# Loading the last w2 row in two partition ranges, without an early write of the output: a decode layer on one Trainium2 core

## The chip, the cores and the metric

The kernel runs on one core of a Trainium2 chip. The metric is the device time of one execution in microseconds, the median of several runs. Beside it there is one profiled execution, from which all durations and positions below are taken.

## The reference

One token each for two batch rows (B = 2, D = 576). The row is normalised, an attention over the last 2048 positions of a cache and a squared-ReLU MLP work on the same normalised row, and both results are added to the input. All tensors are bf16.

```python
xn = layernorm(A_x)                                    # [2, 1, 576]
q  = xn @ wq                                           # 32 heads of 128
p  = softmax(q . k_cache[:, :, -2048:] * 128 ** -0.5)  # 16 kv heads, 2 query heads each
a  = (p . v_cache[:, :, -2048:]) @ wo                  # [4096 x 576]
h  = relu(xn @ w1 + b1) ** 2                           # 4608 wide
m  = h @ w2 + b2                                       # w2: [4608 x 576]
out = A_x + a + m                                      # [2, 1, 576]
```

With two rows there is next to no reuse of weights or cache: 53.6 MB go from HBM to SBUF once, and 2.3 KB come back.

## The kernel before

All large loads are issued by SP, in one order written out by hand: wq, then the k and v tiles of eight units of work (four kv heads of one batch row each, 2 MB a tile), w1 among them, then wo and w2. A load is [128 partitions x n], and each partition's n elements are contiguous in HBM. For each unit the kernel transposes k on TensorE, computes scores, a softmax, and the product with v; the MLP's first half runs when w1 is there (`mlp_h`), and leaves its result transposed in `hT_sb`.

w2 has 4608 rows. They are split into two halves (x = 0, 1) of 128 x 18: partition p holds 18 consecutive rows (FR = 18) of each half, one row being 576 elements or 1152 bytes. The first half is loaded whole into `w2a_sb` (L440), of the second half rows 0 to 8 into `w2b_sb` (L441) and rows 9 to 17 into `w2c_sb` in three pieces given by `W2P`: rows 9 to 14, rows 15 and 16, and row 17 (L442 and L443). All of these are issued by SP between 96 and 101 us. Ahead of them on the queue are the last v tiles and wo, and behind them on SP is only half of the output. A transfer may have to wait before its issue until the one that used its semaphore before has landed.

The end of the kernel is the sum for the output. TensorE accumulates it in `out_ps` (rows 0 and 1: columns 0 to 287; rows 32 and 33: columns 288 to 575): the products with wo, with w2a, then with w2b (18 matmuls), three matmuls into `spin_ps` whose result is not used, and 18 matmuls with w2c. Two matmuls belong to each row of the 18. The first matmul on each piece of w2c waits for that piece.

ScalarE then casts `out_ps` to bf16 (`fin_sb`, L478), and two transfers of [2 x 288] write it out: columns 0 to 287 from ScalarE's queue (L479), columns 288 to 575 from SP's (L480). Ahead of the cast ScalarE issues one more transfer (L477): it writes two partitions of `w2b_sb` to the columns 0 to 287 of the output, as soon as w2b has landed. The real write of L479 goes to the same place and waits until the early one has landed.

Of the kernel before, what the change touches and what calls it, by code (L numbers as in the profile page):

```python
# [16 lines left out]
def kernel(  # L17
# [14 lines left out]
    nc = tc.nc  # L32
    P = 128
    B, Sq, D = A_x.shape
# [39 lines left out]
    FR = L1 // P  # L74
    assert HW == 32 * FR and QH * 2 == NC and NC * WC == 32
    W2P = [(9, 15), (15, 17), (17, 18)]
    R9 = 9
    HD = D // 2
    RO = 32 + B
    RP = 96 + B  # L80
# [11 lines left out]
    def matmul(*a, **k):  # L92
        tc.keep_in_program_order(nc.tensor.matmul(*a, **k))  # L93
# [5 lines left out]
    out2d = out.rearrange("b s d -> (b s) d")  # L99
# [80 lines left out]
    for t0, half, k0, n, pc in ((0, 0, 0, NK, 0), (0, 1, 0, NK, 1), (1, 0, 1, NK - 1, 1), (1, 1, 0, NK - 1, 0)):  # L180
# [11 lines left out]
                          in_=own[:].unsqueeze(2).to_broadcast([P, NC, WC]))  # L192
# [11 lines left out]
                          in_=ident[0:2 * NG4, 0:2 * NG4].rearrange("p (x g) -> p x g", g=NG4).unsqueeze(3)  # L204
# [3 lines left out]
    w2_rows = B_w2.rearrange("(x p r) n -> x p (r n)", x=2, r=FR)  # L208


    w2c_sb = w2pool.tile([P, (FR - R9) * D], BF16, name="w2c")

    out_ps = psum.tile([RO, HD], F32, tag="out", name="out_ps")
    nc.vector.memset(out_ps[:], 0.0)

    def out_acc(lhsT, rhs, o, start=False, stop=False, acc=out_ps, base=0):
        for i in range(2):
            p = base + 32 * i
            matmul(acc[p:p + B, :], lhsT=lhsT, rhs=rhs[:, o * D + i * HD:o * D + (i + 1) * HD], start=start,
                   stop=stop, skip_group_check=True, tile_position=(0, p))  # L220
# [167 lines left out]
    def step(u):  # L388
        fin = None
        w = u - 2  # L390
        with_pv = w >= 0
        for g in range(NG):
            transposes(u, g)
            if with_pv and g == 1:
                pv(w, 0, 2)
            if with_pv and g == 2:
                pv(w, 1, 2)
                fin = pv_end(w)
            if g == TG + 1:
                scores(u, 0)  # L400
            if g == TG + 2 and fin:
                fin()
        scores(u, 1)
        softmax(u)

    def pv_all(u):
        pv(u, 0, 1)
        pv_end(u)()
# [29 lines left out]
    w2a_sb = w2pool.tile([P, FR * D], BF16, name="w2a")  # L438
    w2b_sb = kvpool.tile([P, R9 * D], BF16, tag="kv", name="w2b")
    nc.sync.dma_start(out=w2a_sb[:], in_=w2_rows[0])  # L440
    nc.sync.dma_start(out=w2b_sb[:], in_=w2_rows[1, :, 0:R9 * D])  # L441
    for r0, r1 in W2P:  # L442
        nc.sync.dma_start(out=w2c_sb[:, (r0 - R9) * D:(r1 - R9) * D], in_=w2_rows[1, :, r0 * D:r1 * D])  # L443
    step(NU - 1)
    pv_all(NU - 2)
    pv_all(NU - 1)
    pre_ps = psum.tile([RP, HD], F32, tag="sc", bufs=2, name="pre_ps")
    nc.vector.memset(pre_ps[:], 0.0)
    pre_sb = work.tile([P, HD], F32, tag="t1", name="pre_sb")
    nc.gpsimd.memset(pre_sb[:], 0.0)  # L450
# [17 lines left out]
    for r in range(FR):  # L468
        w, o = (w2b_sb, r) if r < R9 else (w2c_sb, r - R9)
        out_acc(hT_sb[:, 1, r, :], w, o, stop=(r == FR - 1))  # L470
        if r == R9 - 1:
            for _ in range(3):
                matmul(spin_ps[0:B, :], lhsT=ws[:, 0, :], rhs=wo_sb[:, 0:512], start=True, stop=True,
                       skip_group_check=True)

    fin_sb = work.tile([RO, HD], BF16, tag="fin", name="fin_sb")
    nc.scalar.dma_start(out=out2d[:, 0:HD], in_=w2b_sb[0:B, 0:HD])  # L477
    nc.scalar.copy(out=fin_sb[:], in_=out_ps[:])  # L478
    nc.scalar.dma_start(out=out2d[:, 0:HD], in_=fin_sb[0:B, :])  # L479
    nc.sync.dma_start(out=out2d[:, HD:D], in_=fin_sb[32:RO, :])  # L480
# [30 lines left out]
```

## Time and profile before

| What | Value |
|---|---|
| Time, median of 3 runs | 133.66 us (133.63 to 133.71) |
| Profiled execution | 133.6 us, span 131.7 us |
| TensorE busy | 84.6 us (64% of the span) |
| VectorE busy | 63.1 us (48%) |
| ScalarE busy | 46.6 us (35%) |
| Read from HBM | 53.62 MB, 407 GB/s over the span |
| SP's queue (q1) | 95.6% of the 16 DMA engines' time |
| Mean granted TensorE clock | 0.883 |

The span runs from the first to the last instruction of the core. The DMA lines count what the core's 16 DMA engines did; q1 is SP's queue, q10 ScalarE's, and q8 and q14 bring instructions. "Landing" is the update of a transfer's semaphore, which each engine that took part in the transfer makes once. In the lists, "PE" is TensorE, "PEld" its weight loads, "ACTq" and "SPq" the issuing sides of ScalarE and SP.

### The profile page before, as it was taken

The numbers are of one execution on the slowest core, as the hardware profiler recorded it, in microseconds if no ns is written. First come the engines' busy times: TensorE is split into PE (matmuls) and PEld (weight loads), VectorE is DVE, ScalarE is ACT, GpSimd is POOL, SyncE is SP. The second block draws the span as 40 slices with busy tenths as digits, with TensorE's granted clock in tenths as the row PEclk, the third lists the DMA queues.
The fourth block names the chain that finished last, engine by engine and source line by source line (L and its number), as shares of the span: only waits on it lengthen the run. The fifth ranks groups of instructions, "written<-read, shape, count | busy, mean of one in ns | idle before, by whom it ended". The sixth has DMA issues, their size and how long they took to land.

```text
span 131.7 us, 2025 instructions
## 1 busy us (share of the span) xinstructions
PE 84.6 (64%) x818; PEld 46.3 (35%) x818; DVE 63.1 (48%) x176; ACT 46.6 (35%) x68; POOL 4.2 (3%) x14
## 2 busy tenths in 40 slices
PE   0040767985599687699687797003919974629782
PEld 0010236553346353345353353002507631205341
DVE  6760034555447677457677496400073487560000
ACT  6700019497255185265085283200015452000101
POOL 2000000010100100100100100100010001000000
PEclk9999999999779999859999999955586899655799
DMA  4999999999999999999999999999999989899970
GB/s 118 480 419 420 418 443 418 448 418 423 445 413 438 423 443 428 413 458 413 443 423 411 458 490 403 408 431 428 413 443 418 504 381 504 382 416 403 400 286 1
DMA packets 3643, 53.74 MB, mean 408 GB/s; under 512 B 418, under 2 KB 563, under 8 KB 819
## 3 DMA queue, kind: packets, MB, share of 16 engines
q1 hardware_dynamic: 3604, 53.61, 95.6%
q8 instruction: 6, 0.10, 0.3%
q10 hardware_dynamic: 30, 0.02, 0.0%
q14 instruction: 3, 0.02, 0.0%
HBM read 53.62 MB, written 0.00 MB: 407 GB/s over the span
## 4 chain that ended last, share of the span: by engine, by line
DMA 74%; PE 15%; ACT 5%; issue 1%; SPq 1%; DVE 1%; ACTq 0%; DVEq 0%
DMA w<-in_B_w_dram 24%; DMA w2c<-in_B_w_dram 23%; DMA k<-in_A_k_cache_dram 17%; DMA wq<-in_A_wq_dram 10%; PE kT_ps L96 5%; PE h_ps L93 3%; ACT kT L273 3%; PE q_ps L93 2%; PE sc_ps L93 2%; PE o_ps L93 1%; PE out_ps L93 1%; ACT L305 1%; SPq L120 1%; DVE qrow L241 1%; ACT qrow L241 0%
## 5 line engine op out<-in xcount | busy, mean ns | idle before, releaser
L96 PE MATMUL kT_ps<-ident_f,k 128*128 128x128 f32 x256 | 39.0, 295 | 6.7 <-DMA k<-in_A_k_cache_dram 4.2
L273 ACT COPY kT<-kT_ps 128x1024 bf16<-128x1024 bf16 x32 | 31.8, 1012 | 15.3 <-PE kT_ps L96 15.3
L96 PEld LDWEIGHTS kT_ps<-ident_f,k 128*128 128x128 f32 x256 | 29.3, 149 | 21.8 <-issue 7.4
L275 DVE COPY kT<-kT_ps 128x1024 bf16<-128x1024 bf16 x32 | 21.8, 682 | 6.4 <-PE kT_ps L96 5.9
L93 PE MATMUL sc_ps<-kT,qz 128*32 128x512 bf16 x128 | 9.8, 384 | 6.1 <-DVE kT L275 5.5
L305 ACT ACTIVATE p<-sc_ps,bias 128x512 bf16<-128x512 f32 x8 | 5.5, 687 | 21.5 <-DVE gown L301 21.4
L93 PE MATMUL o_ps<-v,pT 128*32 128x512 bf16 x128 | 12.2, 466 | 0.0
L93 PE MATMUL h_ps<-w,xnT 128*4 128x288 bf16 x72 | 4.5, 442 | 8.8 <-DMA w<-in_B_w_dram 8.8
L93 PEld LDWEIGHTS <-xnT 128*4 128x4 bf16 x108 | 3.5, 117 | 18.3 <-issue 15.3
L336 DVE SCALAR_TENSOR_TENSOR o<-o_ps,in_s,o 128x128 f32<-128x128 f32 x24 | 8.2, 344 | 0.4
L308 DVE STREAM_TRANSPOSE pT<-p 128x512 bf16<-128x512 bf16 x8 | 5.7, 709 | 5.6 <-ACT p L305 5.6
L376 DVE TENSOR_TENSOR hrow<-t 100x1152 bf16<-100x1152 f32 x2 | 2.6, 1354 | 10.5 <-ACT t L374 10.5
L93 PE MATMUL q_ps<-wq,xnT 128*4 128x512 bf16 x36 | 4.2, 622 | 5.4 <-DMA wq<-in_A_wq_dram 4.0
L294 DVE TENSOR_REDUCE m<-sc_ps 128x1 f32<-128x512 f32 x8 | 5.5, 691 | 3.4 <-PE sc_ps L93 3.4
L93 PE MATMUL op_ps<-o,of_h 128*32 128x129 f32 x16 | 3.4, 299 | 4.6 <-DVE o L336 4.6
L298 POOL PARTITION_ALL_REDUCE gmax<-m x8 | 2.9, 365 | 92.2 <-DVE m L296 92.2
L93 PEld LDWEIGHTS <-qz 128*32 128x32 bf16 x128 | 2.0, 94 | 9.9 <-DVE kT L275 7.6
L334 DVE TENSOR_SCALAR o<-o_ps,in_s 128x128 f32<-128x128 f32 x8 | 2.7, 343 | 5.3 <-PE o_ps L93 5.3
L96 PE MATMUL pro_ps<-ident,xn_sb 2*128 2x2 bf16 x5 | 0.9, 181 | 6.8 <-DVE xn_sb L171 6.5
L241 ACT CAST qrow<-q_ps 100x512 bf16<-100x512 f32 x1 | 0.6, 585 | 12.1 <-DVE qrow L241 12.1
L463 ACT COPY pre_sb<-pre_ps 34x288 f32<-34x288 f32 x1 | 0.4, 393 | 12.6 <-PE pre_ps L93 12.6
L93 PE MATMUL out_ps<-wo,ws 128*2 128x288 bf16 x32 | 4.0, 441 | 1.1 <-DVE ws L352 1.1
(76 smaller groups left out, 61.4 us busy)
## 6 DMA issues: line engine op xcount, KB each, us to landing
k<-in_A_k_cache_dram SPq DMA_DIRECT2D x8, 2048.0 KB, 25.6
v<-in_A_v_cache_dram SPq DMA_DIRECT2D x8, 2048.0 KB, 22.8
w<-in_B_w_dram SPq DMA_DIRECT2D x1, 5184.0 KB
wo<-in_A_wo_dram SPq DMA_DIRECT2D x1, 4608.0 KB
wq<-in_A_wq_dram SPq DMA_DIRECT2D x1, 3584.0 KB, 12.9
w2a<-in_B_w_dram SPq DMA_DIRECT2D x1, 2592.0 KB
w2b<-in_B_w_dram SPq DMA_DIRECT2D x1, 1296.0 KB, 29.2
wq<-in_A_wq_dram SPq DMA_DIRECT2D x1, 1024.0 KB, 4.8
```

The source lines that it names most:

```text
L93: tc.keep_in_program_order(nc.tensor.matmul(*a, **k))
L96: tc.keep_in_program_order(nc.tensor.transpose(*a, **k))
L241: cp(out=qrow[:, k * QW:(k + 1) * QW].rearrange("p (i a d) -> p i a d", a=2, d=Dh), in_=q_ps[0:RB, k * QW // 2:(k + 1) * QW // 2].rearrang ...
L273: nc.scalar.copy(out=kT, in_=kT_ps[:])
L275: nc.vector.tensor_copy(out=kT, in_=kT_ps[:])
L294: nc.vector.tensor_reduce(out=m1[:], in_=sc_ps[:], axis=AX.X, op=ALU.max)
L298: nc.gpsimd.partition_all_reduce(gmax[:], m2[:], channels=P, reduce_op=ReduceOp.max)
L305: nc.scalar.activation(out=p_sb[:], in_=sc_ps[:], func=ACT.Exp, bias=bias[:, 0:1], scale=scale, accum_out=o1[:, Dh:Dh + 1])
L308: nc.vector.transpose(out=pT[:].rearrange("p j r -> p (j r)"), in_=p_sb[:])
L334: nc.vector.tensor_scalar(scalar1=in_s[:, 0:1], scalar2=None, op0=ALU.mult, **kw)
L336: nc.vector.scalar_tensor_tensor(scalar=in_s[:, k:k + 1], in1=o1[:, 0:Dh], op0=ALU.mult, op1=ALU.add, **kw)
L376: nc.vector.tensor_tensor(out=h4[:, :, k * HB:(k + 1) * HB], in0=t4, in1=t4, op=ALU.mult)
```

## The change

Row 17 of w2c, the last piece, is loaded by two transfers: partitions 0 to 57 and partitions 58 to 127. The other pieces stay as they are. The early write of the output (L477) is left out, so ScalarE issues one transfer less and its write of the output waits for the cast alone.

```diff
     W2P = [(9, 15), (15, 17), (17, 18)]
     R9 = 9
+    PE2 = 58
...
     for r0, r1 in W2P:
-        nc.sync.dma_start(out=w2c_sb[:, (r0 - R9) * D:(r1 - R9) * D], in_=w2_rows[1, :, r0 * D:r1 * D])
+        cols = slice((r0 - R9) * D, (r1 - R9) * D)
+        for p0, p1 in ((0, PE2), (PE2, P)) if r1 == FR else ((0, P),):
+            nc.sync.dma_start(out=w2c_sb[p0:p1, cols], in_=w2_rows[1, p0:p1, r0 * D:r1 * D])
...
     fin_sb = work.tile([RO, HD], BF16, tag="fin", name="fin_sb")
-    nc.scalar.dma_start(out=out2d[:, 0:HD], in_=w2b_sb[0:B, 0:HD])
     nc.scalar.copy(out=fin_sb[:], in_=out_ps[:])
```

In the order of the built program the lists of VectorE and GpSimd are the same as before. SP has one more transfer (58 x 576 and 70 x 576 in place of 128 x 576), and ScalarE one less. On TensorE the order is the same; the first matmul on row 17 waits for the 58 partitions, and the weight load ahead of it for the 70.

## The prediction

> **What bounds the kernel now.** I read the chain that ended last first. Its last pieces, from 95 us on, end in the transfers of w2c:
>
> ```profile
> 96.95 30.81 DMA w2c<-in_B_w_dram
> 127.75 0.04 issue
> 127.80 1.36 PE out_ps L93 x18
> 129.16 0.02 issue
> 129.18 0.39 ACT fin_sb L478
> ```
>
> The reader should see that nothing but weights holds the end: transfers, 18 matmuls on w2c, one ScalarE copy, output. The chain hides one thing: the 18 matmuls have three waits, one for each piece of w2c. In the trace the last two start at 128.85, right behind the last landing of the last piece (128.81), and everything after that is fixed: the copy at 129.18, the two output transfers at 129.60.
>
> ```profile
> 125.71 0.25 ACTq L477 DMA_DIRECT2D out_dram<-w2b  x1
> 129.18 0.39 ACT L478 CAST fin_sb<-out_ps 34x288 bf16<-34x288 f32 x1 [4.37 <-PE out_ps L93]
> 129.60 0.32 SPq L480 DMA_DIRECT2D out_dram<-fin_sb  x1
> 129.60 0.25 ACTq L479 DMA_DIRECT2D out_dram<-fin_sb  x1
> ```
>
> ScalarE's output transfer lands at 130.71, SP's at 130.89, and the span ends at 131.7 behind SP's. So a delay of the last landing of w2c moves the end one for one. Next I asked how full the transfer engines are while that last piece comes in:
>
> ```profile
> core 0: us, PE busy (x) PEld busy (x) DVE busy (x) ACT busy (x) POOL busy (x), PEclk, DMA share, GB/s
> 126.00:126.60 0.60, 0.60 (x16) 0.43 (x12) 0.00 (x0) 0.00 (x0) 0.00 (x0) 1.00 1.02 409
> 126.60:127.10 0.50, 0.50 (x10) 0.29 (x5) 0.00 (x0) 0.00 (x0) 0.00 (x0) 1.00 0.70 275
> 127.10:127.60 0.50, 0.50 (x3) 0.12 (x2) 0.00 (x0) 0.00 (x0) 0.00 (x0) 1.00 0.46 176
> 127.60:128.10 0.50, 0.34 (x7) 0.23 (x7) 0.00 (x0) 0.00 (x0) 0.00 (x0) 1.00 0.37 141
> 128.10:128.50 0.40, 0.40 (x10) 0.29 (x7) 0.00 (x0) 0.00 (x0) 0.00 (x0) 1.00 0.22 78
> ```
>
> The last two columns are the point: the share of the 16 DMA engines falls from all of them to about half at 127.1 and a fifth at 128.3. The engines do not finish together. The trace records every DMA packet, and packets follow each other on an engine without a gap, so the end can be laid out in 16 rows. Each engine moves 8 rows of the last piece, 1152 bytes each, one every 47.0 ns. Eight engines end them between 126.65 and 127.04 us. The other eight end at 127.53, 127.59, 128.09, 128.24, 128.31, 128.42, 128.44 and 128.48. The lag comes from instruction blocks:
>
> ```profile
> q8 instruction: 6, 0.10, 0.3%
> q14 instruction: 3, 0.02, 0.0%
> ```
>
> Six blocks of 16 KB and two of 8 KB (the third record of q14 is a small one) are fetched between 28.9 and 123.3 us. Before the first, 16 landings of one transfer lie within 0.4 us (28.22 to 28.64). After it one of 16 is 1.5 us behind (35.00 against at most 33.49), and each further block makes one more engine late: by about 0.75 us for 8 KB, 1.25 to 1.7 for 16 KB.
>
> **Part 1, the last row in two transfers.** How many engines does a transfer use? Every transfer lands once for each engine: 128 rows give 16 landings, the 4-row loads of b1 give 4, the 2-row transfers 2, the 1-row load of b2 1. In all of them each engine has the same number of rows. I take equal shares as the rule for the new ones. 58 is 2 x 29, so 58 rows in equal shares fit on 2 engines at most (of 16); 70 is 14 x 5, so 70 rows go on 14. The trace names no engines, and I assume that transfers on two engines always have the same two, which the 14 include.
>
> The Trainium skill says the same in "DMA: Bandwidth & Descriptors", section "Why a DMA increments its semaphore by 16 and not by 1": the engine count is the largest number up to 16 that divides the slowest dimension, and on this path the lowest-numbered engines are taken. By it 58 goes on engines 0 and 1, and 70 on 0 to 13; no transfer of 58 or 70 rows is in the trace to agree or not.
>
> So two engines have 29 + 5 = 34 rows of the last piece instead of 8, twelve have 5, two have none. Which two get 34? The early write of the output is a 2-row transfer, and its packets show them. One is at 126.764 us, directly behind the packet that ends the last piece on an engine that is on time (126.76); the other is at 127.534, directly behind the end at 127.53 us. So one of the two is on time, and the other is the least late of the eight.
>
> - The late one of the two: 26 rows more x 0.047 = 1.22 us, and one more semaphore write, 0.006 us. 127.53 + 1.23 = 128.76 us. From the last byte to the landing the trace has 0.28 to 0.38 us, 0.30 on this engine. Landing at 129.06 (129.04 to 129.14).
> - The on-time one: 126.76 + 1.23 = 127.99 us, covered.
> - The other late ones: 3 rows less x 0.047 = 0.14 us. 128.48 - 0.14 = 128.34 us, landing at 128.67. No longer last.
>
> The last landing goes from 128.81 to 129.06: **+0.25 us** (0.23 to 0.33). The gain of 0.14 us on the twelve is paid for and lost, because the two that take over the work have only one free member.
>
> The additional transfer costs SP one more issue, 0.33 to 0.43 us by the row of line 443, at about 97 us; nothing is queued behind it on SP but the final output at 129.60, and the queue then holds 25 us of work. Cost nothing. On TensorE the last row now has two waits, one on a weight load (70 rows, landing 128.67) and one on the matmul behind it (58 rows). Nothing else is queued there, and the weight load is under the longer wait. Rows 15 and 16 keep their landing, 128.46, and their four matmuls end before 129.
>
> **Part 2, no early write.** It is issued in 4.4 us of ScalarE idleness (the bracket in the second fence), and its packets (29 + 9 ns) come after the last piece on both engines. Removing it frees nothing on the path. The final write of ScalarE also no longer waits for its landing at 128.00; that wait was over before 129.60. Gain: none.
>
> What may be lost is a warmed path. ScalarE's final write goes from packet to landing in 0.36 us; the early pair took 0.47, and SP's final one 0.49. If ScalarE's becomes like these, it lands 0.12 later, at 130.83, still ahead of SP's 130.89: nothing. The far bound is the first transfer that queue makes, the load of x: 1.49 us from issue to landing, against 1.11 for the final write. That is 0.38, less 0.18 of cover by SP: 0.20 us. I take 0.03, near the first, since the early write's issue (0.25 us) was no longer than the final one's.
>
> **Sum.** +0.25 + 0.03 = +0.28 us. The profiled execution took 133.6 us, 0.06 below the median of the runs, 133.66; the sum gives 133.88 for it and 133.94 for the median. That is 0.21%, just about the 0.2% (0.27 us) that a measurement of this kernel can tell from no change.
>
> **Rivals.**
> 1. *Blocks fall on other engines, and the two are on time.* That each block is tied to a fixed engine is not shown; the trace is one execution. If both of the two end their 8 rows before 128.34 - 1.23 = 127.11 us, the split does only good: every late engine has 3 rows less, the last landing is 0.14 earlier, 133.52 us. For it: 8 of 16 engines are on time. Against: the TensorE and VectorE programs, which need most blocks, keep their length (1217 rows and 152), and the runs of before lie within 0.08 us.
> 2. *Blocks of 16 KB fall on one of the two.* Then 34 rows begin on an engine that ends at 128.09 to 128.48: 129.32 to 129.71, +0.8 to +1.2 us, 134.5 to 134.9. The same against it.
> 3. *The halves are spread over all engines anyway.* With uneven shares an engine would have at most 4 + 5 = 9 rows instead of 8: +0.047 us, 133.7. Only rows in equal shares are in the trace, which speaks against it. The Trainium skill, in the same page, "Rules for kernel authors", says of two transfers to disjoint partition halves: "Don't bother — they serialize", as both spread over the same engines. By that rule the two would take the time of one and the result would be no change; the trace has no such pair to test it.
>
> **How the numbers follow.** My forecast 0.66, rival 1 0.13, rival 2 0.13, rival 3 0.08. The forecast's own range is 0.23 to 0.33 and 0 to 0.20 on top, 133.89 to 134.19; six parts in ten of it lie over 0.27 us, as the cold write can only add. So slower 0.66 x 0.62 + 0.13 = 0.54; rival 1 gives at most 0.14 us, which is within 0.2%, and I keep 0.05 for a gain that I don't see; the rest, 0.41, is no change. The range takes in rivals 1 and 3 and leaves out rival 2: 133.50 to 134.20.
>
> **What would show it.** In the profile of the changed kernel: the wait of the last two matmuls ends at about 129.1, not 128.85. The stretch from 128.5 to 128.75 has one engine busy, a share near 0.06, where before it had none. The 58-row transfer has 2 landings and the 70-row one 14; the 14 are all in by 128.7. ScalarE's write lands at most 0.2 us later against its issue, SP's as before. Wrong would be: 16 landings of either half (rival 3); both landings of the 58 rows ahead of the 14 (rival 1); one of the two past 129.5 (rival 2); an unchanged last landing with a later end (the early write mattered).

## The result, and the profile after

The changed kernel takes 133.97 us (median of 12 runs, 133.81 to 134.28), the one before 133.63 (12 runs, 133.47 to 133.80). The ratio is 1.0026, with a 95% interval of 1.0019 to 1.0033: +0.34 us, slower. The profiled execution took 133.87 us with a span of 132.0, against 133.6 and 131.7. One execution of the kernel before (159.1 us) and one of the kernel with 28 additional rows below (247.64 us) were far slower than the rest and are in no ratio; the second was the one profiled, so that kernel ran again for its trace.

The chain that ended last, changed kernel (start, length, what):

```profile
96.95 31.04 DMA w2c<-in_B_w_dram
127.99 0.04 issue
128.03 1.35 PE out_ps L94 x18
129.38 0.02 issue
129.41 0.39 ACT fin_sb L480
```

Up to the issue of w2c it is the chain of before within 0.01 us. The first piece of w2c lands 0.24 us later (127.99 against 127.75), and the cast starts 0.23 later (129.41 against 129.18). The end in order of time:

```profile
128.03 1.33 PE L94 MATMUL out_ps<-w2c,hT_sb 128*2 128x288 bf16 x18 [0.38 <-DMA w2c<-in_B_w_dram]
129.07 0.08 PEld L94 LDWEIGHTS <-hT_sb 128*2 128x2 bf16 x2 [0.16 <-DMA w2c<-in_B_w_dram]
129.41 0.39 ACT L480 CAST fin_sb<-out_ps 34x288 bf16<-34x288 f32 x1 [4.81 <-PE out_ps L94]
129.82 0.25 SPq L482 DMA_DIRECT2D out_dram<-fin_sb  x1
129.83 0.25 ACTq L481 DMA_DIRECT2D out_dram<-fin_sb  x1
```

The early write is gone, and the second line is new: the weight load for row 17 waits for the 70 rows. The share of the DMA engines, and the GB/s that they moved, are again the last two columns:

```profile
126.60:127.10 0.50, 0.50 (x10) 0.29 (x5) 0.00 (x0) 0.00 (x0) 0.00 (x0) 1.00 0.69 263
127.10:127.60 0.50, 0.50 (x3) 0.13 (x2) 0.00 (x0) 0.00 (x0) 0.00 (x0) 1.00 0.44 166
127.60:128.10 0.50, 0.12 (x3) 0.06 (x3) 0.00 (x0) 0.00 (x0) 0.00 (x0) 1.00 0.48 182
128.10:128.50 0.40, 0.40 (x8) 0.28 (x9) 0.00 (x0) 0.00 (x0) 0.00 (x0) 1.00 0.22 75
128.50:128.75 0.25, 0.25 (x8) 0.17 (x3) 0.00 (x0) 0.00 (x0) 0.00 (x0) 1.00 0.03 9
```

From 127.6 to 128.1 more of the engines are at work than before (0.48, was 0.37): by the packets, both engines with 34 rows are still moving them, where before they had ended by 127.53. From 128.50 on a single engine is left for half of the stretch. Before, there was none:

```profile
128.50:128.75 0.25, 0.25 (x8) 0.20 (x4) 0.00 (x0) 0.00 (x0) 0.00 (x0) 1.00 0.00 0
```

The end of the two profiled executions by the trace, in us:

| | before | after |
|---|---|---|
| last landing, rows 9 to 14 | 127.75 | 127.99 |
| last landing, rows 15 and 16 | 128.46 | 128.78 |
| last landing, row 17 | 128.81 | 129.03 (58 rows: 128.85) |
| last pair of matmuls starts | 128.85 | 129.07 |
| output lands, ScalarE / SP | 130.71 / 130.89 | 131.10 / 130.94 |
| SP is through its last waits | 130.97 | 131.25 |

The sum of +0.28 us has two parts: 0.22 up to the last matmuls, and 0.06 behind the output's landing.

### The profile page after: what moved, and what is told of

Read it like the earlier page. It is cut to its first block, busy times and chain, and to the rows that moved or that the text cites. A ratio compares the mean times of both kernels' runs of the same rounds, so it can differ in the third digit from the quotient of the medians.

```text
span 132.0 us, 2024 instructions
## 1 busy us (share of the span) xinstructions
PE 84.4 (64%) x818; PEld 46.1 (35%) x818; DVE 63.2 (48%) x176; ACT 46.7 (35%) x68; POOL 4.2 (3%) x14
## 4 chain that ended last, share of the span: by engine, by line
DMA 75%; PE 13%; ACT 5%; SPq 2%; issue 1%; DVE 1%; ACTq 0%; DVEq 0%
DMA w<-in_B_w_dram 25%; DMA w2c<-in_B_w_dram 24%; DMA k<-in_A_k_cache_dram 17%; DMA wq<-in_A_wq_dram 10%; PE kT_ps L97 4%; PE h_ps L94 3%; ACT kT L274 3%; PE q_ps L94 2%; PE sc_ps L94 2%; PE out_ps L94 1%; ACT L306 1%; PE o_ps L94 1%; SPq L121 1%; DVE qrow L242 1%; ACT qrow L242 0%
## 5 line engine op out<-in xcount | busy, mean ns | idle before, releaser
L242 DVE CAST qrow<-q_ps 100x512 bf16<-100x512 f32 x1 | 0.7, 691 | 8.3 <-PE q_ps L94 8.3
```

What stands on the lines that cost most here:

```text
L242: cp(out=qrow[:, k * QW:(k + 1) * QW].rearrange("p (i a d) -> p i a d", a=2, d=Dh), in_=q_ps[0:RB, k * QW // 2:(k + 1) * QW // 2].rearrang ...
```

## The experiments

Every ratio is to the runs of the kernel before on the same chip, with its 95% interval. Two ideas were open after the result. The *share theory* is the prediction's: two engines carry 34 rows. But the table shows something it doesn't explain: rows 9 to 16, whose transfers were not changed, land 0.24 to 0.32 later. The second idea is *collisions*: a transfer of a part of the partitions slows what other engines still have in flight. Each trace is one execution, and where it lies far from the median of its runs, this is said.

**One part at a time.** The split alone:

```diff
-        nc.sync.dma_start(out=w2c_sb[:, (r0 - R9) * D:(r1 - R9) * D], in_=w2_rows[1, :, r0 * D:r1 * D])
+        cols = slice((r0 - R9) * D, (r1 - R9) * D)
+        for p0, p1 in {17: ((0, 58), (58, 128))}.get(r0, ((0, P),)):
+            nc.sync.dma_start(out=w2c_sb[p0:p1, cols], in_=w2_rows[1, p0:p1, r0 * D:r1 * D])
```

> Row 17 in partitions 0 to 57 and 58 to 127, the early write of the output kept. Share theory (58 rows go on two engines, and the later of the two ends last): the last pair of matmuls starts at about 129.07 us as in the changed kernel, 0.22 later than before (128.85), and the time is 133.63 + 0.22 to 0.28 = 133.85 to 133.91. Theory that the early write matters (its absence is what costs): no more than 0.05 over before, 133.68. The 58 rows land twice, the 70 rows 14 times.

Measured: 133.94 us, ratio 1.0028 (1.0019 to 1.0037). The split alone is the whole of the slowdown within the intervals. The 58 rows land twice, at 128.26 and 129.09, the 70 rows 14 times, the last at 129.31 alone (the one ahead is at 128.91). The traced execution took 134.09 us, 0.15 over the median:

```profile
105.48 23.83 DMA w2c<-in_B_w_dram
129.31 0.04 issue
129.35 0.31 PE out_ps L93 x2
129.66 0.02 issue
129.69 0.39 ACT fin_sb L480
```

The chain now goes through the last pair of matmuls only (x2), and the transfer ahead of it is that of the 70 rows, issued at 105.48. In this execution the later of the two engines ends its 34th row at 128.88, 0.47 behind the next one.

**The early write alone left out**, twice:

```diff
-    nc.scalar.dma_start(out=out2d[:, 0:HD], in_=w2b_sb[0:B, 0:HD])
```

> Row 17 in one transfer as before, the early write of the output left out. Share theory: the last pair of matmuls starts at 128.85 as before, and the time is that of before, 133.63, or up to 0.06 more if ScalarE's write now lands behind SP's, as in the changed kernel (131.10 against 130.94). Theory that the early write matters: +0.25 to +0.35, 133.9 to 134.0, with a longer way from the issue of ScalarE's write (129.60) to its landing than the 1.11 us of before.

> The kernel without the early write alone once more, since its interval in the first round of experiments (1.0000 to 1.0018) leaves open if there is a price. No price: an interval around 1.0000 to 1.0005, and both together under 1.001. A price of about 0.12 us: 1.0009 again.

Measured: 133.74 us, ratio 1.0009 (1.0000 to 1.0018), and 133.75 us, 1.0007 (0.9998 to 1.0015): about 0.1 us in both, at the edge of either interval. The trace has a place for 0.06 us of it. From the start of the cast to the last landing it takes 1.72 and 1.73 us in the two, 1.71 before and 1.70 in the changed kernel, so no path got colder. But SP waits at the end for the transfers' semaphores one after another, always in the same order. Before, the last write to land uses the last semaphore in that order: SP is through 0.08 us behind the landing. A transfer less moves both writes one semaphore ahead; one more wait follows the landing, and SP is through 0.14 us behind it in both runs, +0.06. In the changed kernel SP's write keeps the last semaphore, but ScalarE's lands last, and the wait for SP's comes behind it: 0.14 again. That ScalarE's write comes second there goes with this split: it does so in the split alone too (131.38 against 131.20), and not in these two runs.

**A split with equal work for all engines:**

```diff
...
+        for p0, p1 in {17: ((0, 64), (64, 128))}.get(r0, ((0, P),)):
...
```

> Row 17 in partitions 0 to 63 and 64 to 127, the early write kept. Share theory: 64 rows go on 16 engines, 4 rows each, so every engine still moves 8 rows; 16 landings for either half, the last near 128.81 plus one more semaphore write of 0.006, and the time of before, 133.63 (within 0.05). Theory that a second transfer and a second wait cost by themselves: most of the 0.25 to 0.34 is there again, 133.9.

Measured: 133.99 us, ratio 1.0033 (1.0020 to 1.0046). The share theory expected nothing here, and this is as slow as the change. (0.10 us of it are two more waits of SP behind the landing; 0.3 lie ahead of it.) Both halves land 16 times, so every engine does have its 4 + 4 rows. The trace (of the slowest of the five executions, 134.26) shows what else happened: rows 9 to 14, loaded as before, end their landing at 128.23 instead of 127.75.

```profile
127.10:127.60 0.50, 0.50 (x3) 0.14 (x2) 0.00 (x0) 0.00 (x0) 0.00 (x0) 1.00 0.41 137
127.60:128.10 0.50, 0.06 (x1) 0.00 (x0) 0.00 (x0) 0.00 (x0) 0.00 (x0) 1.00 0.42 161
128.10:128.50 0.40, 0.23 (x4) 0.17 (x5) 0.00 (x0) 0.00 (x0) 0.00 (x0) 1.00 0.40 135
128.50:128.75 0.25, 0.25 (x8) 0.17 (x4) 0.00 (x0) 0.00 (x0) 0.00 (x0) 1.00 0.18 60
```

From 127.1 to 127.6 the engines are as busy as before but for 0.05, yet they move 137 GB/s instead of 176. Packets of 6912 bytes, always 262 ns from 126 us on before, now take 279 to 416 ns in 14 cases, all between 126.5 and 127.4: just when the engines that are on time write row 17 to 64 partitions and the late ones are still writing rows 9 to 14 to all 128. In the changed kernel five such packets take 274 to 345 ns, in the split alone five (291 to 372).

**A smaller share of the two engines:**

```diff
...
+        for p0, p1 in {17: ((0, 38), (38, 128))}.get(r0, ((0, P),)):
...
```

> Row 17 in partitions 0 to 37 and 38 to 127, the early write kept. Share theory: 38 rows go on 2 engines (19 each), 90 rows on 15 (6 each). The later one of the two has 25 rows, 17 more than before: 127.53 + 0.80 = 128.33, landing at 128.63 to 128.73; the other late engines have 2 rows less, 128.48 - 0.09 = 128.39, landing at about 128.72. So the last landing is 0.08 earlier than before, and the time 133.55. Theory that rows written by two engines into partitions that are otherwise other engines' disturb these (in the changed kernel the two rows ahead landed at 128.78 instead of 128.46): the landing of rows 15 and 16 is late again by 0.2 to 0.3, and the time is 0.05 to 0.2 above before.

Measured: 133.80 us, ratio 1.0015 (1.0006 to 1.0024). Slower, so the small gain that the share theory expected is not seen. The landings are 2 and 15, as equal shares want. Rows 15 and 16 land at 128.59, 0.13 later than before. The two engines with 25 rows don't set the end: the 38 rows are in by 128.39, and the last of the 90 lands at 128.85. Only one packet of 6912 bytes is longer (299 ns). The last packet of all ends at 128.37, as the share theory has it (128.39; before 128.49), but its landing comes 0.48 us behind it instead of 0.33, and the gain is gone. The traced execution, 133.63, is the fastest of the eleven, so where the +0.2 of the median lies it doesn't show.

**Two transfers without partitions being split**, and **partitions split without a half left out**:

```diff
+        for c0, c1 in ((r0 * D, r0 * D + HD), (r0 * D + HD, r1 * D)) if r1 == FR else ((r0 * D, r1 * D),):
+            nc.sync.dma_start(out=w2c_sb[:, c0 - R9 * D:c1 - R9 * D], in_=w2_rows[1, :, c0:c1])
```

> Row 17 in two transfers by columns: 128 partitions x 288 elements twice, 8 packets of 576 bytes for each engine and transfer; early write kept. Theory that a second transfer and its semaphore cost by themselves (what the 64/64 split could mean, +0.40): +0.3 to +0.4, 133.9 to 134.0. Theory of collisions (a transfer of part of the partitions sends 16 engines to the few partitions that the late engines are still writing; packets of 6912 bytes then take 290 to 416 ns instead of 262): all engines write their own 8 partitions as in a whole transfer, so no packet of rows 9 to 14 is longer than 266 ns, the price is 16 x about 0.026 instead of 8 x 0.047, +0.04, and the time 133.63.

```diff
...
+        for pp in (slice(0, P, 2), slice(1, P, 2)) if r1 == FR else (slice(0, P),):
+            nc.sync.dma_start(out=w2c_sb[pp, cols], in_=w2_rows[1, pp, r0 * D:r1 * D])
```

> Row 17 in two transfers by partitions, the even ones and then the odd ones, 64 rows each; early write kept. Each engine moves 4 + 4 rows, as with the 64/64 split, but either transfer reaches all of the 128 partitions' range instead of one half of it. Theory of collisions by half of the range: packets of rows 9 to 14 on the late engines stay near 262 ns, at most a few over 290, and the time is within 0.1 of before, 133.6 to 133.7. Theory that any second transfer over partitions costs: 133.9 to 134.0 again.

Measured: by columns 133.78 us, ratio 1.0008 (0.9999 to 1.0017); by even and odd partitions 133.80 us, 1.0008 (0.9999 to 1.0016). Both are +0.1 us, and no packet of rows 9 to 16 is longer than before. In both SP has two more waits behind the landing and is through 0.19 us behind it (before 0.08): 0.10 us, which is what was measured. So a second transfer as such costs next to nothing beyond its semaphore, and 64 rows spread over the whole range of partitions don't collide, while 64 rows in one half do.

**More pieces of the range:**

```diff
...
+        for p0, p1 in {17: ((0, 32), (32, 64), (64, 96), (96, 128))}.get(r0, ((0, P),)):
...
```

> Row 17 in four transfers of 32 partitions, 2 rows for each engine and transfer; early write kept. Share theory: 8 rows for each engine as before, four semaphore writes of 0.006 instead of one: 133.65. Theory of collisions: 16 engines go to a quarter of the partitions at a time; packets of rows 9 to 14 and 15 to 16 on the late engines are longer than nominal as in the 64/64 split or more, +0.3 to +0.8, 133.9 to 134.4.

Measured: 134.47 us, ratio 1.0058 (1.0044 to 1.0072), +0.78. Nine packets of 6912 bytes take 271 to 400 ns. Of the 0.78, three more waits behind the landing are 0.17 (0.25 against 0.08). The traced execution, the fastest of the six (134.22), has the rest of its own +0.61: the last packet ends 0.10 later than before (128.59 against 128.49), and the last landing comes 0.67 behind it instead of 0.33.

**Behind the last packet.** Longer packets are thus the smaller part of what collisions do in most of these traces. The larger part lies between the last packet of a transfer (on each engine that is one of 4 bytes behind its data, which writes the semaphore) and its last landing, on rows 9 to 16, which were loaded in the same way in every run:

| row 17 | rows 9 to 14: last packet, last landing | between | rows 15 and 16: last packet, last landing | between |
|---|---|---|---|---|
| whole (before) | 127.38, 127.75 | 0.37 | 128.11, 128.46 | 0.35 |
| two halves of the columns | 127.47, 127.82 | 0.35 | 128.19, 128.54 | 0.35 |
| even and odd partitions | 127.51, 127.91 | 0.40 | 128.23, 128.61 | 0.38 |
| 58 and 70, changed kernel | 127.44, 127.99 | 0.55 | 128.16, 128.78 | 0.62 |
| 58 and 70, split alone | 127.43, 127.98 | 0.56 | 128.17, 128.71 | 0.54 |
| 38 and 90 | 127.33, 127.86 | 0.53 | 128.09, 128.59 | 0.51 |
| 64 and 64 | 127.61, 128.23 | 0.61 | 128.46, 129.03 | 0.57 |
| four quarters | 127.46, 127.95 | 0.49 | 128.19, 128.64 | 0.45 |

In the other five traces with row 17 whole it is 0.33 to 0.42. So the two groups don't overlap: 0.33 to 0.42 us where row 17 comes whole or in parts that each reach over the whole range of partitions, 0.45 to 0.62 where it comes in pieces of the range. In the changed kernel the last packets of rows 9 to 16 end only 0.05 to 0.06 us later than before; nearly all of the 0.24 and 0.32 by which their landings are late is this longer way.

**The two engines' load by itself.** Row 17 in one transfer, and ahead of it 28, 14 or 42 rows' worth for the two engines alone, into a tile that is not used:

```diff
+    more_sb = kvpool.tile([P, 14 * D], BF16, tag="kv", name="more")
     for r0, r1 in W2P:
+        if r1 == FR:
+            for p, n in ((0, 14), (1, 14)):
+                nc.sync.dma_start(out=more_sb[p:p + 5:4, 0:n * D], in_=w2_rows[0, p:p + 5:4, 0:n * D])
```

> Row 17 in one transfer as before, early write kept; ahead of it two additional transfers of 2 partitions x 16128 bytes (28 rows in all) of the first half of w2 into a tile that is not used, so only the two engines of the small transfers have more to do: 2 x about 0.60 us = 1.20, near the 26 rows x 0.047 = 1.22 of the change. Share theory: the later of the two ends at 127.53 + 1.20 = 128.73, landing about 129.05, the last pair of matmuls starts at 129.08 and the time is 133.59 + 0.23 = 133.82 (133.75 to 133.95). If the two engines' load decides nothing and collisions alone make the change slower: within 0.08 of before, 133.55 to 133.67, with the last landing at 128.8.

> Row 17 in one transfer, early write kept, and ahead of it one additional transfer of 2 partitions x 14 rows instead of two. Share theory: 0.60 us more on the two engines; the later one ends at 127.53 + 0.60 = 128.13, ahead of the latest of the others (128.48), so the time is that of before within 0.1. Theory that an additional small transfer costs by itself: half of the +0.32 that two of them cost, +0.16.

> The same with three additional transfers of 14 rows. Share theory: 1.80 us more on the two engines; the later one ends at 127.53 + 1.80 = 129.33, landing at 129.63 to 129.73, 0.8 to 0.9 later than before, and from the second transfer on each 14 rows cost their full 0.60: +0.8 to +0.95 over before. Theory that an additional small transfer costs by itself: three times 0.16, +0.48.

| rows for each of the two | time, us | ratio (interval) | SP through behind the last landing, us |
|---|---|---|---|
| + 14 | 133.82 | 1.0009 (1.0001 to 1.0018) | 0.19 |
| + 28 | 134.05 | 1.0024 (1.0015 to 1.0033) | 0.25 |
| + 42 | 134.72 | 1.0078 (1.0064 to 1.0092) | 0.32 |

The medians are 0.18, 0.37 and 1.08 us over before (133.64, 133.68, 133.64). Take off what the waits at the end add over 0.08 us, by one trace of each (0.10, 0.17, 0.24), and 0.08, 0.20 and 0.84 remain. The first 14 rows cost next to nothing, the next ones a part, the last ones their full 0.60. That is a load that has slack first and then decides, as the share theory has it (0, 0.23, 0.8 to 0.95), and not a price for each transfer. With 42 rows the chain shows it:

```profile
122.57 7.04 DMA w2c<-in_B_w_dram
129.60 0.04 issue
129.65 0.31 PE out_ps L93 x2
```

15 of the 16 landings of row 17 are in by 129.01, and one stands alone at 129.60. In the three traces (the 28 rows' from the run below) no packet of rows 9 to 16 is longer than before.

> The kernel with 28 additional rows for the two engines once more, for its trace. Share theory: the last transfer of w2c lands 16 times; 15 landings by 128.9 and one alone at 129.0 to 129.15, and the last pair of matmuls starts right behind it; packets of rows 9 to 16 keep 262 and 93 ns, and rows 15 and 16 land by 128.6. Collisions: longer packets again, and no landing that stands alone.

The kernel with 28 rows once more, 133.96 us in its one run (before 133.47), for the trace. It was half a miss: the late one of the two lands at 129.01, inside the range expected, but it doesn't stand alone. Another engine is at 128.99, since in this execution all the late engines were late (rows 15 and 16 by 128.63). One trace can't divide 0.02 us from 0.2; the medians do.

## Why the prediction was right

The forecast was 133.94 and +0.28; measured were 133.97 and +0.34, and in the profiled executions +0.27.

- *Equal shares: right.* 58 rows land twice, 70 rows 14 times, 38 twice, 90 15 times, and by the packets two engines move 29 + 5 rows and two move none of row 17. The trace agrees with the Trainium skill's "DMA: Bandwidth & Descriptors", section "Why a DMA increments its semaphore by 16 and not by 1".
- *One of the two on time, one the least late: right, and it holds from run to run.* In the changed kernel they end their 34 rows at 128.13 and 128.63. The forecast had 127.99 and 128.76. Wherever the early write is there to show the two engines, the instruction blocks have left one on time and made the other a little late, so rivals 1 and 2 were not seen.
- *The last landing at 129.06: 129.03.* The last pair at about 129.1: 129.07. The size of this step is right, and part of that is luck. The later of the two engines was through 0.13 us earlier than forecast, and the way from its last packet to the landing took about 0.40 us instead of 0.30 (0.36 if its landing is the one at 128.99), so two misses nearly cancel. With 0.30 the load of the two engines would have given 128.93, 0.12 later than before (an estimate from these two numbers).
- *"Rows 15 and 16 keep their landing, 128.46": wrong.* They land at 128.78, and their four matmuls keep TensorE until the very moment at which row 17 is there. The prediction put the effect of the split on other transfers at nothing, without a reason. Two causes end at the same place here: the share (129.03) and the collisions. In the split alone, the share was 0.4 behind the next; in the 64/64 split the last pair of matmuls starts 0.56 later than before without any share, in an execution 0.27 over its median. The prediction got the size with one of two mechanisms, because they run side by side and don't add up.
- *0.14 us less for the other late engines, landing at 128.67: wrong at the landing.* Their last packets end at 128.40 instead of 128.49, but the last two landings of the 70 rows are at 128.99 and 129.03. The trace names no engine for a landing, but only one of the two engines with 34 rows is busy past 128.40, and the other, through at 128.13, would need 0.86 us for either landing. So one of the two is all but surely that of an engine with 5 rows, about 0.6 us behind its last packet. "No longer last" holds by 0.04 us at most. The 38/90 split, which by shares alone would have been faster, didn't show this gain either.
- *The early write, +0.03 for a colder path: right in size, wrong in kind.* No path is colder; ScalarE's write takes 1.28 us from issue to landing against 1.11, but SP's takes 1.11 against 1.29: whichever comes second takes longer, and their order changed. What the removal is seen to cost is the order of the last waits, 0.06 us.
- *"0.33 to 0.43 us" for SP's further issue: wrong, without consequence.* The issue of the 70 rows behind the 58 took 6.22 us (100.75 to 106.97), and 1.73 us in the split alone. Nothing was queued behind it on SP until 129.82, as the prediction said.
- *Rival 3* (the halves spread over all engines anyway) did not come about, by the landings. The advice it rests on, "Don't bother", in the Trainium skill's "DMA: Bandwidth & Descriptors", section "Rules for kernel authors", holds all the same. Here the reason is stronger: a split into halves of the range is not neutral, but 0.4 us slower, 0.3 of it ahead of the last landing.

What stays open: why a transfer to a part of the partitions slows the packets in flight and delays their landings. The runs show that 64 rows in half of the range do it and 64 rows over the whole range don't; a path to each group of partitions that several engines share would fit, and was not tried by itself. Nor do the runs tell the writes to SBUF from the reads of HBM: half of the partitions is also half of w2's rows there. No version run here beats the kernel before.

## What to carry to other kernels

Where loads set the end, look at all 16 landings of the last transfers, not at the last one: who is late, by how much, and which engines a transfer with another number of rows will use. Change the number of rows of a late transfer only with its divisors in mind, and keep it over the whole range of partitions, since here a part of the range delayed the other engines' transfers. Compare the end of the last packet with the landing: a transfer can lose its time between the two. When a change moves the time by 0.1 us, look at which semaphore the last transfer signals before looking for a mechanism.

## What was not expected of the hardware

- SP's waits at the end cost 0.06 us each if they come behind the last landing: SP was through 0.08 us after it with one wait left, 0.14 with two, 0.19 with three, 0.25 with four, 0.32 with five. An additional transfer anywhere can shift this.
- A packet of 6912 bytes took up to 416 ns instead of 262 while other engines moved 64 neighbouring rows.
- The last landing of a transfer came 0.45 to 0.62 us behind its last packet, instead of 0.33 to 0.42, when the row behind it was loaded in pieces of the partition range, even where no packet or only one was longer.
- Behind a transfer of 58 rows on two engines the next issue on SP took 6.22 us in the changed kernel and 1.73 in the split alone, instead of 0.33 to 0.43.
- The early write on ScalarE's queue was issued at 125.71 and moved only when the engine had ended its packets from SP's queue, at 126.764 and 127.534. With the split its two landings came at 128.68 and 129.48. Only in the kernel with 42 additional rows did one engine move it (129.03) with two packets of row 17 still to come.
